# Chunked attention and a gated network: the next block's attention in two batches instead of four

## The chip, the cores and the metric

The kernel runs on one core of one Trainium2 chip. The metric is the time of one launch on the device in microseconds (us), lower is better. The engines that matter are TensorE (PE, matrix products into PSUM), VectorE (DVE), ScalarE (ACT) and the queues on which DMAs are issued: SyncE's (SP) for loads, and ACT's own for the output.

## The reference

Attention within chunks of 64 positions, for 8 batches, 8 heads, 576 positions and 64 numbers a head, then a gated feed-forward network on 4608 tokens of 512 numbers:

```python
scores = scale * np.matmul(q_c, k_c.transpose(0, 1, 2, 4, 3))
scores = scores - np.max(scores, axis=-1, keepdims=True)
attn = np.exp(scores)
attn = attn / (np.sum(attn, axis=-1, keepdims=True) + 1e-09)
out = np.matmul(attn, v_c)
...
g = x @ w_gate
silu = g * (1.0 / (1.0 + np.exp(-g)))
val = x @ w_val
return (silu * val @ w_out).astype(np.float32)
```

`w_gate` and `w_val` are 512 x 1536, `w_out` is 1536 x 512.

## The kernel before

The tokens are taken in nine blocks (b = 0 to 8) of 512. A block's attention covers four pairs of heads (p = 0 to 3). `Attn` holds it: `load_qk` loads a pair's q and k, `scores` (L180) makes their products in two PSUM tiles (h = 0, 1; a PSUM tile here is one bank of 128 x 512 numbers), takes the maximum of each row and writes the difference to `s` in SBUF, `exponents` (L201) and `normalize` (L206) finish the softmax in place, `turn` (L229) transposes it into the tile `turned` by DVE, `columns_crossed` (L242) multiplies with v into two banks and copies them back to `s` by ACT, and `ready` (L264) splits the result into two parts xh and xl, the operands of the feed-forward network. Each small product is 64 x 64; the program has 32 such instructions for two pairs, and the trace shows 64, since it lists each of these as two passes.

The network runs in twelve steps (f = 0 to 11) of 128 hidden columns. A step of a block is: `gate` (12 large matmuls into a bank of the pool `ps_gv`, silu by ACT, L292), `value` (12 more into the other bank of `ps_gv`), `times` (L299, DVE, reads the value's bank), the splitting of `h` into hh (ACT) and hl (DVE), L56 and L57, and 12 matmuls of `project` (L312) into four banks of `ps_o`. The pool `ps_gv` has two banks, `ps_a` two, `ps_o` four: all eight are taken. A product of three parts stands for each exact one (L273 to L275, L318 to L320). `lag` (L331) runs `project` one step late: the output product of step f-1 is emitted behind the gate and value of step f. So the previous block's step 11 is projected at f = 0 of the next block, and there ACT copies the four output tiles out (L325) and issues their DMAs (L327) on its own queue, each behind its copy.

The order on PE, ACT and DVE is the order in which the code is written. The order of SP's DMAs is set by a scheduler. From b = 2 on, `block` (L558) makes the attention of block b+1 between the steps of block b: `behind[f]` is called at the end of step f, `middle[f]` ahead of step f's output weights. Blocks 2 to 7 do this, six in all; blocks 0, 1 and 2 get their attention elsewhere, in code that the change leaves in its order.

```python
middle = {2: exponents}
behind = {0: lambda: scores(0), 1: lambda: scores(2), 3: normalize,
          4: lambda: turn(0, 0), 5: lambda: turn(0, 1),
          6: lambda: (values(0), turn(2, 0)),
          7: lambda: turn(2, 1), 8: lambda: nxt.ready(0, 2), 9: lambda: values(2), 10: lambda: nxt.ready(2, 2)}
```

`scores(p)` and `values(p)` each handle pairs p and p+1, in the two banks of `ps_a`. The loads of q and k use two buffers, `qk_t`, each for one pair; the staged h tiles of the pass ahead of block 2 (twelve late steps of block 1) use the same two. The v loads and two of the four output tiles share the buffers `v_t`.

Of the kernel before, what the change touches and what calls it, by code (L numbers as in the profile page):

```python
# [8 lines left out]
F32 = mybir.dt.float32  # L9
# [10 lines left out]
P = 128  # L20
C = 64
# [6 lines left out]
NP = H // 2  # L28
T = 4
# [6 lines left out]
def attn_then_gated_ffn(ctx: ExitStack, tc: tile.TileContext, qk, v, wgv, wo, out):  # L36
    nc = tc.nc
    const = ctx.enter_context(tc.tile_pool(name="const", bufs=1))
    ld = ctx.enter_context(tc.tile_pool(name="ld", bufs=2))
# [6 lines left out]
    ps_gv = ctx.enter_context(tc.tile_pool(name="ps_gv", bufs=2, space=bass.MemoryType.PSUM))  # L46
    ps_o = ctx.enter_context(tc.tile_pool(name="ps_o", bufs=T, space=bass.MemoryType.PSUM))
    ps_a = ctx.enter_context(tc.tile_pool(name="ps_a", bufs=2, space=bass.MemoryType.PSUM))
# [106 lines left out]
    class Attn:  # L155
# [12 lines left out]
                              in_=qk[:, p:p + n, self.b].rearrange("p n a k -> p n (a k)"))  # L168
            return t

        def load_v_crossed(self, p):

            t = ld.tile([P, 2, T, C], F32, name="v_t", tag="v_t")
            src = v[:, p, self.b].rearrange("p (c j) d -> p c j d", j=2)
            nc.sync.dma_start(out=t[:, 0], in_=src[:, :, 0])
            for h in range(2):
                nc.sync.dma_start(out=t[h * C:(h + 1) * C, 1], in_=src[(1 - h) * C:(2 - h) * C, :, 1])
            return t

        def scores(self, tiles, p, c=0, m=T, pool=ps_a, tag="ps_a"):  # L180

            n = sum(t.shape[1] for t in tiles)
            ps = [pool.tile([P, n, m, C], F32, name="ps_a", tag=tag) for _ in range(2)]
            i = 0
            for t in tiles:
                for k in range(t.shape[1]):
                    for u in range(2 * m):
                        j, us = u % 2, u % (2 * M) * C
                        for h in range(2):
                            r = slice(h * C, (h + 1) * C)  # L190
                            part = t[r, k, u // (2 * M)]
                            nc.tensor.matmul(ps[h][j * C:(j + 1) * C, i, u // 2, :], part[:, us:us + C],  # L192
                                             part[:, M * P + us:M * P + us + C], start=True, stop=True)
                    i += 1
            for h in range(2):
                top = small.tile([P, n, m, 1], F32, name="top")
                nc.vector.tensor_reduce(out=top, in_=ps[h], axis=AX.X, op=ALU.max)  # L197
                nc.vector.tensor_tensor(out=self.s[:, p:p + n, c:c + m, h], in0=ps[h],
                                        in1=top.broadcast_to([P, n, m, C]), op=ALU.subtract)
# [19 lines left out]
        def columns(self, v_t, pT, pool=ps_a, tag="ps_a"):  # L219

            pT = pT.rearrange("p (u k) -> p u k", k=C)
            px = pool.tile([P, 2 * T, C], F32, name="px", tag=tag)
            for u in range(2 * T):
                for h in range(2):
                    r = slice(h * C, (h + 1) * C)
                    nc.tensor.matmul(px[r, u, :], v_t[r, u, :], pT[r, u, :], start=True, stop=True)  # L226
            return px.rearrange("p u k -> p (u k)")

        def turn(self, p, j, parts=(0, 1)):  # L229


            if not hasattr(self, "turned"):
                self.turned = const.tile([P, NP, 2, T, C], F32, name="turned", tag="turned")
            src = self.s[:, p:p + 2].rearrange("p a c h k -> p (a c) h k")
            for i in (2 * j + i for i in parts):
                for o in range(4):
                    to = 32 * (o ^ 2 * j)
                    nc.vector.transpose(  # L238
                        out=self.turned[to:to + 32, p:p + 2, j, :, 32 * (i % 2):32 * (i % 2) + 32],
                        in_=src[32 * i:32 * i + 32, :, o // 2, 32 * (o % 2):32 * (o % 2) + 32])  # L240

        def columns_crossed(self, v_t, p, n):  # L242


            px = [ps_a.tile([P, n, T, C], F32, name="ps_a") for _ in range(2)]
            for i in range(n):
                for u in range(T):
                    for j in range(2):
                        for h in range(2):
                            r = (h ^ j) * C  # L250
                            nc.tensor.matmul(px[j][h * C:(h + 1) * C, i, u, :], v_t[i][r:r + C, j, u, :],  # L251
                                             self.turned[r:r + C, p + i, j, u, :], start=True, stop=True)
            for j in range(2):
                nc.scalar.copy(out=self.s[:, p:p + n, :, j], in_=px[j])
# [22 lines left out]
    def out_weights(f, engine=None):  # L277
        woh = wp.tile([P, DM], F32R, name="woh")
        wol = wp.tile([P, DM], F32R, name="wol")
        split(wo_raw[f], woh, wol, engine)  # L280
        return woh, wol
# [19 lines left out]
    def gated(a, f):  # L301
        h = gate(a, f)
        times(h, value(a, f))
        return h

    def parts(a, f, h):
        hh = hp.tile([P, N], F32R, name="hh")
        hl = hp.tile([P, N], F32R, name="hl")
        split(h, hh, hl)
        return a, f, hh, hl  # L310
# [20 lines left out]
    def lag(parts, wo_f):  # L331

        if pending:
            project(*pending.pop())
        if parts is not None:
            pending.append((parts, wo_f))

    def side(a):

        kept = {}  # L340

        def scores(p):
            a.scores([a.load_qk(p), a.load_qk(p + 1)], p)

        def exponents():
            kept["s"] = a.exponents(0, NP)

        def normalize():
            a.normalize(kept["s"])

        def turn(p, j, parts=(0, 1)):
            a.turn(p, j, parts)
            if j and 1 in parts:
                kept["v"] = [a.load_v_crossed(p + i) for i in range(2)]

        def values(p):
            a.columns_crossed(kept["v"], p, 2)

        return scores, exponents, normalize, turn, values
# [35 lines left out]
    def by_pe(a, pairs, v_t):  # L395
        for p in pairs:
            a.turn_by_pe(p, turned_by_pe[:, p])
        return [a.columns(v_t[p], turned_by_pe[:, p], ps_o, "ps_o") for p in pairs]
# [8 lines left out]
    px = by_pe(a0, (0, 1), v0)  # L407
# [26 lines left out]
    px = by_pe(a1, (0, 1), v1)  # L434
# [65 lines left out]
    def pT(p):  # L500
        return nxt.turned[:, p].rearrange("p j t k -> p (j t k)")
# [8 lines left out]
    def prepare(f):  # L510
        if f % 2 == 0:
# [14 lines left out]
    o.below()  # L526
    nxt = Attn(2)
    scores, exponents, normalize, turn, values = side(nxt)
    o.power()
    scores(0)  # L530
    o.weigh()
    o.join()
# [15 lines left out]
    behind = {1: lambda: turn(0, 0, (0,)), 2: lambda: (turn(0, 0, (1,)), nxt.turn_by_pe(2, pT(2))),  # L548
              3: lambda: (turn(0, 1, (0,)), columns(2), nxt.turn_by_pe(3, pT(3))),
              4: lambda: (columns(3), turn(0, 1, (1,))), 5: lambda: nxt.ready(2, 2),  # L550
              6: lambda: values(0), 8: lambda: nxt.ready(0, 2)}
# [6 lines left out]
    def block(a, b):  # L558
        nxt = Attn(b + 1) if b + 1 < NB else None
        middle, behind = {}, {}  # L560
        if nxt:
            scores, exponents, normalize, turn, values = side(nxt)
            middle = {2: exponents}
            behind = {0: lambda: scores(0), 1: lambda: scores(2), 3: normalize,
                      4: lambda: turn(0, 0), 5: lambda: turn(0, 1),
                      6: lambda: (values(0), turn(2, 0)),
                      7: lambda: turn(2, 1), 8: lambda: nxt.ready(0, 2), 9: lambda: values(2), 10: lambda: nxt.ready(2, 2)}
        for f in range(NF):
            wo_f = []

            def between():
                middle.get(f, lambda: None)()
                wo_f.extend(out_weights(f))

            h = gated(a, f)
            between()
            lag(parts(a, f, h), wo_f)
            behind.get(f, lambda: None)()
        return nxt

    a = nxt
    for b in range(2, NB):
        a = block(a, b)
# [34 lines left out]
```

## Time and profile before

| | us |
|---|---|
| median of 3 runs | 989.31 (988.85 to 989.68) |
| the profiled execution | 988.99 |
| its span, first to last instruction | 987.1 |
| PE busy in it | 952.7 |
| DVE busy | 513.5 |
| ACT busy | 337.7 |

The chain of work that ended last lies on PE for 91% of the span. The granted clock of PE has a mean of 0.991. A busy PE is not proof of PE at its peak, since matmuls are pipelined and overlap in the trace (a large one is listed with 0.39 us); the starts tell how far they stand apart.

### The profile page before, as it was taken

Reading aid. Unit: us, or ns where it says so; the run is one execution under the profiler, and the core shown is the slowest. Engines: PE = TensorE matmul, PEld = TensorE weight load, DVE = VectorE, ACT = ScalarE, POOL = GpSimd, SP = SyncE. Lnnn points to the kernel's source line nnn. Section 1 sums busy time; section 2 is a strip of 40 time slices with the busy share of each in tenths; the row PEclk is TensorE's granted clock in tenths of the full one; section 3 lists DMA queues with packets and bytes.
Section 4 is the critical chain, followed back from the end, with each engine's and each line's share of the span. In section 5 each row is a group of like instructions: output and inputs, shape, how many; then the busy total and the mean of one; then the engine's idle time right before and its main releaser. Section 6 shows DMA issues by size and latency. Waiting matters only on the chain.

```text
span 987.1 us, 14517 instructions
## 1 busy us (share of the span) xinstructions
PE 952.7 (97%) x6232; PEld 782.2 (79%) x6232; DVE 513.5 (52%) x816; ACT 337.7 (34%) x523; POOL 0.7 (0%) x6
## 2 busy tenths in 40 slices
PE   4689999999999999999999999999999999999998
PEld 4577888876888888888888888888888888888886
DVE  6777777758447524662356345633564347522221
ACT  3455444434532223222332323233322332223222
POOL 0000000000000000000000000000000000000000
PEclk9799999999999999999999999999999999999999
DMA  9061333235240005010401030002100120001001
GB/s 362 14 234 38 134 147 141 92 112 160 80 136 1 22 1 150 1 23 1 150 0 23 1 112 39 22 1 92 58 20 4 29 79 1 22 1 43 0 1 43
DMA packets 45600, 63.85 MB, mean 65 GB/s; under 512 B 29664, under 2 KB 29664, under 8 KB 44000
## 3 DMA queue, kind: packets, MB, share of 16 engines
q1 hardware_dynamic: 38624, 50.34, 15.8%
q10 hardware_dynamic: 6912, 12.59, 3.4%
q8 instruction: 49, 0.80, 0.3%
q14 instruction: 15, 0.12, 0.0%
HBM read 50.33 MB, written 12.58 MB: 64 GB/s over the span
## 4 chain that ended last, share of the span: by engine, by line
PE 91%; DVE 4%; DMA 2%; ACT 2%; issue 1%; ACTq 0%; SPq 0%; DVEq 0%
PE ps_gv L273 20%; PE ps_gv L274 19%; PE ps_gv L275 19%; PE ps_o L318 9%; PE ps_o L319 9%; PE ps_o L320 9%; DMA qk_t<-in_qk 2%; PE ps_a L192 2%; PE ps_a L251 1%; PE px L226 1%; DVE z L208 1%; DMA out<-o_sb 0%; DVE s_sb L211 0%; DVE t L81 0%; DVE t L97 0%
## 5 line engine op out<-in xcount | busy, mean ns | idle before, releaser
L273 PE MATMUL ps_gv<-xl,w 128*128 128x512 f32 x864 | 341.1, 395 | 3.4 <-ACT h L292 2.1
L274 PE MATMUL ps_gv<-xh,w 128*128 128x512 f32 x864 | 338.1, 391 | 3.2 <-DVE w L129 3.2
L275 PE MATMUL ps_gv<-xh,w 128*128 128x512 f32 x864 | 337.9, 391 | 0.0
L299 DVE SCALAR_TENSOR_TENSOR h<-ps_gv,h 128x512 f32<-128x512 f32 x108 | 74.6, 690 | 359.3 <-PE ps_gv L275 359.3
L273 PEld LDWEIGHTS ps_gv<-xl,w 128*128 128x128 f32 x864 | 163.0, 189 | 39.3 <-ACT h L292 2.5
L274 PEld LDWEIGHTS ps_gv<-xh,w 128*128 128x128 f32 x864 | 163.1, 189 | 36.9 <-DVE w L129 3.8
L275 PEld LDWEIGHTS ps_gv<-xh,w 128*128 128x128 f32 x864 | 163.0, 189 | 34.2
L292 ACT ACTIVATE h<-ps_gv 128x512 f32<-128x512 f32 x108 | 64.5, 597 | 315.0 <-PE ps_gv L275 314.9
L318 PE MATMUL ps_o<-woh,hl 128*128 128x512 f32 x432 | 169.9, 393 | 2.2 <-DVE hl L57 2.1
L319 PE MATMUL ps_o<-wol,hh 128*128 128x512 f32 x432 | 169.0, 391 | 0.0
L320 PE MATMUL ps_o<-woh,hh 128*128 128x512 f32 x432 | 168.9, 391 | 0.0
L56 ACT CAST hh<-h 128x512 fp32r<-128x512 f32 x96 | 59.6, 621 | 183.4 <-DVE h L299 183.4
L318 PEld LDWEIGHTS ps_o<-woh,hl 128*128 128x128 f32 x432 | 81.5, 189 | 21.1 <-issue 2.5
L319 PEld LDWEIGHTS ps_o<-wol,hh 128*128 128x128 f32 x432 | 81.6, 189 | 17.1 <-DVE wol L57 0.4
L320 PEld LDWEIGHTS ps_o<-woh,hh 128*128 128x128 f32 x432 | 81.5, 189 | 17.0
L238 DVE STREAM_TRANSPOSE turned<-s_sb 32x256 f32<-32x256 f32 x208 | 90.6, 436 | 3.1
L57 DVE TENSOR_TENSOR wol<-wo,woh 128x512 fp32r<-128x512 f32 x108 | 73.8, 683 | 12.8 <-ACT woh L56 12.8
L57 DVE TENSOR_TENSOR hl<-h,hh 128x512 fp32r<-128x512 f32 x96 | 66.4, 692 | 18.1 <-ACT hh L56 11.1
L56 ACT CAST woh<-wo 128x512 fp32r<-128x512 f32 x108 | 66.0, 611 | 11.1 <-DVE wo L97 11.1
L197 DVE TENSOR_REDUCE top<-ps_a 128x8 f32<-128x512 f32 x36 | 24.6, 685 | 36.1 <-PE ps_a L192 36.1
L192 PEld LDWEIGHTS ps_a<-qk_t 64*64 64x64 f32 x1152 | 20.4, 144 | 14.8 <-DMA qk_t<-in_qk 9.2
L192 PE MATMUL ps_a<-qk_t 64*64 64x64 f32 x1152 | 23.5, 232 | 8.8 <-DMA qk_t<-in_qk 8.4
(49 smaller groups left out, 438.7 us busy)
## 6 DMA issues: line engine op xcount, KB each, us to landing
qk_t<-in_qk SPq DMA_DIRECT2D x30, 512.0 KB, 4.5
raw<-in_wgv SPq DMA_DIRECT2D x12, 1024.0 KB, 7.0
out<-o_sb ACTq DMA_DIRECT2D x36, 256.0 KB, 2.3
raw<-in_wo SPq DMA_DIRECT2D x6, 1024.0 KB, 4.9
v_t<-in_v SPq DMA_DIRECT2D x26, 128.0 KB, 2.8
v_t<-in_v SPq DMA_DIRECT2D x52, 64.0 KB, 2.8
qk_t<-in_qk SPq DMA_DIRECT2D x3, 1024.0 KB, 13.8
h<-h ACTq DMA_DIRECT2D x12, 256.0 KB, 2.0
```

The source lines that it names most:

```text
L56: nc.scalar.copy(out=hi, in_=src)
L57: (engine or nc.vector).tensor_tensor(out=lo, in0=src, in1=hi.bitcast(F32), op=ALU.subtract)
L192: nc.tensor.matmul(ps[h][j * C:(j + 1) * C, i, u // 2, :], part[:, us:us + C], part[:, M * P + us:M * P + us + C], start=True, stop=True)
L238: nc.vector.transpose(out=self.turned[to:to + 32, p:p + 2, j, :, 32 * (i % 2):32 * (i % 2) + 32], in_=src[32 * i:32 * i + 32, :, o // 2, 3 ...
L273: nc.tensor.matmul(ps, wh, xl, start=k == 0, stop=False)
L274: nc.tensor.matmul(ps, wl, xh, start=False, stop=False)
L275: nc.tensor.matmul(ps, wh, xh, start=False, stop=k == n - 1)
L292: nc.scalar.activation(h, pg, AF.Silu, scale=2.0 ** -8)
L299: nc.vector.scalar_tensor_tensor(out=h, in0=pv, scalar=2.0 ** -8, in1=h, op0=ALU.mult, op1=ALU.mult)
L318: nc.tensor.matmul(o, hl[:, ts], woh, start=f == 0, stop=False)
L319: nc.tensor.matmul(o, hh[:, ts], wol, start=False, stop=False)
L320: nc.tensor.matmul(o, hh[:, ts], woh, start=False, stop=f == NF - 1)
```

## The change

In `block`, the scores of all four pairs are made at f = 0, and their values at f = 8. Pairs 0 and 1 use the two banks of `ps_gv`, pairs 2 and 3 those of `ps_a`. The scores in `ps_gv` are copied to `s` by ACT (`take`) and reduced from there; those in `ps_a` are reduced from PSUM as before. Pairs 2 and 3 of q and k are loaded by one DMA into the buffer of `turned`, and v of pairs 2 and 3 into the two buffers `qk_t`, both at other times of the block than their usual holders.

```diff
+        def take(self, ps, p):
+            to = [self.s[:, p:p + ps[0].shape[1], :, h] for h in range(2)]
+            for h in range(2):
+                nc.scalar.copy(out=to[h], in_=ps[h])
+            return to
...
-        def columns_crossed(self, v_t, p, n):
-            px = [ps_a.tile([P, n, T, C], F32, name="ps_a") for _ in range(2)]
+        def columns_crossed(self, v_t, p, n, pool=ps_a, tag="ps_a"):
+            px = [pool.tile([P, n, T, C], F32, name="ps_a", tag=tag) for _ in range(2)]
...
-            scores, exponents, normalize, turn, values = side(nxt)
+            _, exponents, normalize, _, _ = side(nxt)
+            kept_v = []
+            def scores():
+                tiles = [nxt.load_qk(0), nxt.load_qk(1)], [nxt.load_qk(2, 2, const, "turned")]
+                ps = nxt.products(tiles[0], pool=ps_gv, tag="ps_gv"), nxt.products(tiles[1])
+                nxt.less_top(nxt.take(ps[0], 0), 0)
+                nxt.less_top(ps[1], 2)
+            def load_v():
+                kept_v.extend(nxt.load_v_crossed(p, "v_t" if p < 2 else "qk_t") for p in range(NP))
+            def values():
+                nxt.columns_crossed(kept_v[:2], 0, 2, ps_gv, "ps_gv")
+                nxt.columns_crossed(kept_v[2:], 2, 2)
             middle = {2: exponents}
-            behind = {0: lambda: scores(0), 1: lambda: scores(2), 3: normalize,
-                      4: lambda: turn(0, 0), 5: lambda: turn(0, 1),
-                      6: lambda: (values(0), turn(2, 0)),
-                      7: lambda: turn(2, 1), 8: lambda: nxt.ready(0, 2), 9: lambda: values(2), 10: lambda: nxt.ready(2, 2)}
+            behind = {0: scores, 3: normalize, 4: lambda: turn(0, 0), 5: lambda: turn(0, 1),
+                      6: lambda: (turn(2, 0), load_v()), 7: lambda: turn(2, 1),
+                      8: values, 9: lambda: nxt.ready(0, 2), 10: lambda: nxt.ready(2, 2)}
```

`products` and `less_top` are the two halves of the former `scores`; `load_v_crossed` takes the buffer's tag as a further argument.

How instructions move on ACT at f = 0 of block 3 (o_sb are the output tiles, h the result of the silu of f = 1, s_sb the scores of block 4; numbers tell buffers apart). Before:

```order
L325 ACTIVATE o_sb_3132<-ps_o_2383 128x512
L327 DMA out_0<-o_sb_3132 128x512
L292 ACTIVATE h_3192<-ps_gv_3179 128x512
L56 CAST woh_3208<-wo1_639 128x512
L56 CAST hh_3212<-h_3192 128x512
```

After:

```order
L339 ACTIVATE o_sb_3132<-ps_o_2427 128x512
L341 DMA out_0<-o_sb_3132 128x512
L204 COPY s_sb_3073<-ps_a_3141 128x8x64
L204 COPY s_sb_3073<-ps_a_3142 128x8x64
L306 ACTIVATE h_3236<-ps_gv_3223 128x512
L56 CAST woh_3252<-wo1_639 128x512
```

The two new copies (their tiles are called ps_a, but lie in `ps_gv`) stand behind the last output tile's copy and DMA issue and ahead of the silu of f = 1.

How they move on PE at the same place, f = 0 of block 3. Before:

```order
L319 MATMUL ps_o<-wol,hh 128x512
L320 MATMUL ps_o<-woh,hh 128x512
L192 MATMUL ps_a<-qk_t 64x64 x32
L273 MATMUL ps_gv<-xl_2875,w 128x512
L274 MATMUL ps_gv<-xh_2874,w 128x512
```

After:

```order
L333 MATMUL ps_o<-wol,hh 128x512
L334 MATMUL ps_o<-woh,hh 128x512
L195 MATMUL ps_a<-qk_t 64x64 x64
L287 MATMUL ps_gv<-xl_2960,w 128x512
L288 MATMUL ps_gv<-xh_2959,w 128x512
```

The batch of 32 has become one of 64, between the same output product and the gate of f = 1; the batch at f = 1 is gone. At f = 8 there is one of 64 too, in place of those at f = 6 and f = 9.

How loads move on SP ahead of block 2 (h_in are the staged h tiles). Before:

```order
L513 DMA h_in_2183<-h10_1672 128x1024
L167 DMA qk_t_2299<-in_qk 128x1024
L167 DMA qk_t_2301<-in_qk 128x1024
L167 DMA qk_t_2396<-in_qk 128x1024
L175 DMA v_t_2659<-in_v 128x4x64
L167 DMA qk_t_2398<-in_qk 128x1024
```

After:

```order
L527 DMA h_in_2183<-h10_1672 128x1024
L167 DMA qk_t_2303<-in_qk 128x2x1024
L167 DMA qk_t_2299<-in_qk 128x1024
L167 DMA qk_t_2301<-in_qk 128x1024
L175 DMA v_t_2724<-in_v 128x4x64
```

Pairs 2 and 3 come as one load, ahead of pairs 0 and 1, and no v load stands between them any more.

More of the change, by code (lines that the diff above doesn't have):

```diff
@@ L169, in load_qk, with load_v_crossed @@
             return t
-        def load_v_crossed(self, p):
-            t = ld.tile([P, 2, T, C], F32, name="v_t", tag="v_t")
+        def load_v_crossed(self, p, tag="v_t"):
+            t = ld.tile([P, 2, T, C], F32, name="v_t", tag=tag)
             src = v[:, p, self.b].rearrange("p (c j) d -> p c j d", j=2)
@@ L180, in scores, with products @@
         def scores(self, tiles, p, c=0, m=T, pool=ps_a, tag="ps_a"):
+            self.less_top(self.products(tiles, c, m, pool, tag), p, c)
+        def products(self, tiles, c=0, m=T, pool=ps_a, tag="ps_a"):
             n = sum(t.shape[1] for t in tiles)
@@ L194, in scores, with less_top @@
                     i += 1
+            return ps
+        def take(self, ps, p):
[3 more added lines that the diff above has]
+            return to
+        def less_top(self, ps, p, c=0):
+            n, m = ps[0].shape[1:3]
             for h in range(2):
@@ L561, in block, with turn @@
         if nxt:
-            scores, exponents, normalize, turn, values = side(nxt)
-            middle = {2: exponents}
-            behind = {0: lambda: scores(0), 1: lambda: scores(2), 3: normalize,
-                      4: lambda: turn(0, 0), 5: lambda: turn(0, 1),
-                      6: lambda: (values(0), turn(2, 0)),
-                      7: lambda: turn(2, 1), 8: lambda: nxt.ready(0, 2), 9: lambda: values(2), 10: lambda: nxt.ready(2, 2)}
+            _, exponents, normalize, _, _ = side(nxt)
[10 more added lines that the diff above has]
+                nxt.columns_crossed(kept_v[2:], 2, 2)
+            middle = {2: exponents}
+            behind = {0: scores, 3: normalize, 4: lambda: turn(0, 0), 5: lambda: turn(0, 1),
+                      6: lambda: (turn(2, 0), load_v()), 7: lambda: turn(2, 1),
+                      8: values, 9: lambda: nxt.ready(0, 2), 10: lambda: nxt.ready(2, 2)}
+            def turn(p, j):
+                nxt.turn(p, j)
         for f in range(NF):
```

## The prediction, made before the changed kernel had run

> **What bounds the kernel now.** I read the page's span and chain first, then the busy time over one block, then the chain in order of time for what repeats in a block, then TensorE's (PE's) own timeline around a batch of small products.
>
> ```profile
> span 987.1 us, 14517 instructions
> PE 91%; DVE 4%; DMA 2%; ACT 2%; issue 1%; ACTq 0%; SPq 0%; DVEq 0%
> ```
>
> The chain that ended last lies on PE for 91% of the span. The view by windows, for one whole block of 512 tokens (first column the stretch, then its length, then the busy time of PE with the number of instructions), shows that inside a block PE has no gap at all:
>
> ```profile
> 374.88:478.08 103.20, 103.20 (x695) 84.91 (x689) 50.32 (x84) 31.79 (x52) 0.00 (x0) 1.00 0.15 42
> ```
>
> DVE (50.32) and ScalarE, called ACT (31.79), have much room. So a block is the sum of PE's pieces, and the change must be read there. The chain in order of time shows the four batches of the next block's attention (start, duration): two of L192 (scores, f=0 and f=1) and two of L251 (values, f=6 and f=9).
>
> ```profile
> 373.85 1.09 PE ps_a L192 x64
> 383.33 1.09 PE ps_a L192 x64
> 425.45 1.09 PE ps_a L251 x64
> 451.25 1.09 PE ps_a L251 x64
> ```
>
> Now PE's timeline at one f=0 (start, duration, line; a duration includes the drain, so I go by starts):
>
> ```profile
> 473.72 0.39 PE L274 MATMUL ps_gv<-xh,w 128*128 128x512 f32 x1
> ...
> 476.67 0.39 PE L320 MATMUL ps_o<-woh,hh 128*128 128x512 f32 x1
> 476.98 1.16 PE L192 MATMUL ps_a<-qk_t 64*64 64x64 f32 x64
> 478.08 0.50 PE L273 MATMUL ps_gv<-xl,w 128*128 128x512 f32 x1
> ...
> 478.88 0.39 PE L273 MATMUL ps_gv<-xl,w 128*128 128x512 f32 x1
> ```
>
> From 473.72 to 476.67 thirteen large matmuls start, 0.227 apart. From the last large one before the batch (476.67, below "t0") to the first behind it (478.08) are 1.41, and the three after that take 0.80 instead of 0.68. So a batch costs 1.41 - 0.227 + 0.12 = 1.30 us. Sum of a block: 432 x 0.227 + 4 x 1.30 = 103.3, against 103.20 in the window. Nothing else is in it.
>
> **What merging saves.** How much of the 1.30 goes away when two batches stand back to back? The first block has a batch that a late load cut in two:
>
> ```profile
> 279.11 0.39 PE L320 MATMUL ps_o<-woh,hh 128*128 128x512 f32 x1
> 279.42 0.69 PE L192 MATMUL ps_a<-qk_t 64*64 64x64 f32 x32
> 280.54 0.69 PE L192 MATMUL ps_a<-qk_t 64*64 64x64 f32 x32 [0.42 <-DMA qk_t<-in_qk]
> 281.16 0.50 PE L273 MATMUL ps_gv<-xl,w 128*128 128x512 f32 x1
> ```
>
> 32 passes take 0.69, 64 take 1.16: 0.47 for 32 more, so 0.94 for 64 more. A batch of 128 costs 1.30 + 0.94 = 2.24 instead of 2.60: 0.36 us saved by each merge. Two merges a block in six blocks (b = 2 to 7; the last has no next block) are 12 x 0.36 = 4.3 us. Bounds: 0.2 to 0.4 each (64 passes that need a whole 1.09 more, or nothing left of the switch but the 0.94).
>
> The same rows give the third term: here 279.11 to 281.16 are 2.05 instead of 1.41, so PE lost 0.64 us to the load of pair 3. Afterwards all loads of that block stand ahead of the v loads in SP's order, and the last of them waits only for the last staged h tile, whose last reader is this row on DVE; a load of 512 KB lands 4.5 us after its issue, one of 1 MB 13.8:
>
> ```profile
> 259.83 0.69 DVE L57 TENSOR_TENSOR hl<-h_in,hh 128x512 fp32r<-128x512 f32 x1 [1.43 <-ACT hh L56]
> ...
> qk_t<-in_qk SPq DMA_DIRECT2D x30, 512.0 KB, 4.5
> ...
> qk_t<-in_qk SPq DMA_DIRECT2D x3, 1024.0 KB, 13.8
> ```
>
> 260.5 + 4.5 = 265, ahead of the batch at 269.9. The 1 MB load is issued before that, when `turned` comes free at the sixth of twelve steps. So 0.64 us is won once. In later blocks the loads are released at f=8, three steps of 8 us before their use, and the v loads at f=0, eight steps ahead: nothing waits.
>
> **What the new place costs.** The first two pairs' products now fill both banks of `ps_gv`. The next gate product (f=1) writes the first of them and must wait until ACT has copied it out. At f=0 ACT also empties the previous block's four output tiles (L325), each followed by a DMA issue on the same queue (L327), and the new copies stand behind all of them. ACT's timeline at the same f=0:
>
> ```profile
> 475.69 0.59 ACT L325 ACTIVATE o_sb<-ps_o 128x512 f32<-128x512 f32 x1
> ...
> 477.48 0.34 ACTq L327 DMA_DIRECT2D out<-o_sb  x1
> 477.92 0.60 ACT L325 ACTIVATE o_sb<-ps_o 128x512 f32<-128x512 f32 x1 [0.47 <-PE ps_a L192]
> 478.55 0.34 ACTq L327 DMA_DIRECT2D out<-o_sb  x1
> 479.06 0.60 ACT L325 ACTIVATE o_sb<-ps_o 128x512 f32<-128x512 f32 x1 [0.55 <-ACT o_sb L325]
> 479.69 0.41 ACTq L327 DMA_DIRECT2D out<-o_sb  x1
> 481.13 0.60 ACT L292 ACTIVATE h<-ps_gv 128x512 f32<-128x512 f32 x1 [1.47 <-PE ps_gv L275]
> ```
>
> The last issue ends at 480.10, t0 + 3.43, long after PE left the output product. Today nothing waits for that: the next thing on ACT is the silu at 481.13. Of the six blocks one is later, with t0 = 373.47 and the last issue over at 377.13, t0 + 3.66; the other five lie close to the first.
>
> ```profile
> 373.47 0.39 PE L320 MATMUL ps_o<-woh,hh 128*128 128x512 f32 x1
> ...
> 376.79 0.34 ACTq L327 DMA_DIRECT2D out<-o_sb  x1
> ```
>
> The copy itself I price by the copy of the same shape (589 ns), and the hand-over from ACT to PE by a place where PE waited for ACT (75.47 to 75.52: 0.05):
>
> ```profile
> L254 ACT COPY s_sb<-ps_a 128x512 f32<-128x512 f32 x26 | 14.0, 589 | 28.7 <-PE ps_a L251 28.7
> ```
>
> ```profile
> 74.87 0.60 ACT h L292
> 75.52 0.50 PE ps_gv L273
> ```
>
> So: 480.10, + 0.10 (from an issue's end to the next ACT instruction that has nothing to wait for, 477.82 to 477.92), + 0.59, + 0.05 = 480.84. Without the wait the gate would start at 478.08 + 0.94 = 479.02. PE stands still 1.82 us; in the late block 377.13 + 0.74 - (373.47 + 2.35) = 2.05. Five times 1.82 and once 2.05 are 11.2 us. Bounds for one wait: 1.6 (no gap, output copies a little earlier) to 2.05. The second copy ends half a microsecond later and serves the value product, 2.7 us behind the gate: no wait.
>
> The same question at f=8, where values of pairs 0 and 1 go to `ps_gv`: there ACT has no output tiles, and starts its copies at once:
>
> ```profile
> 528.58 1.16 PE L251 MATMUL ps_a<-turned,v_t 64*64 64x64 f32 x64
> 529.67 0.50 PE L273 MATMUL ps_gv<-xl,w 128*128 128x512 f32 x1
> ...
> 529.78 1.07 ACT L254 COPY s_sb<-ps_a 128x512 f32<-128x512 f32 x2 [2.39 <-PE ps_a L251]
> ```
>
> The first copy ends at 529.78 + 0.59 = 530.37, and the second half of the batch runs until 529.67 + 0.94 = 530.61. Covered by 0.2 us, so nothing; that cover is thin.
>
> DVE takes on no more instructions than before, only all at f=0. A pair's four (two reductions, two subtractions) took 478.20 to 480.93:
>
> ```profile
> 478.20 0.69 DVE L197 TENSOR_REDUCE top<-ps_a 128x8 f32<-128x512 f32 x1 [1.69 <-PE ps_a L192]
> ...
> 480.24 0.69 DVE L198 TENSOR_TENSOR s_sb<-ps_a,top 128x512 f32<-128x512 f32 x1
> ```
>
> Two such groups from 480.8 end at 486.2; the gated product that DVE makes next needs the value product of f=1, which ends at about 480.84 + 24 x 0.227 = 486.3, and the output product that reads it stands two more products away. Hidden. The turns, which now end at f=7, have all of f=8's gate and value ahead of the batch. The 12 more copies on ACT (two a block) cost PE nothing but the wait above.
>
> **Sum.** - 4.3 - 0.64 + 11.2 = + 6.2 us. The profiled execution took 988.99 us (span 987.1); the median of the runs shown is 989.31, 0.3 above. 989.3 + 6.2 = 995.5 us.
>
> **The clock.** PE's clock is the first rival. The windows view around two gaps, cut into stretches of 3.41 us such that the halved one is whole (behind the length the busy time of PE; third from the end, 1.00 or 0.50, the granted clock):
>
> ```profile
> 71.65:75.07 3.42, 1.76 (x8) 1.13 (x6) 2.70 (x6) 1.73 (x4) 0.00 (x0) 1.00 0.00 0
> 75.07:78.48 3.41, 2.96 (x13) 2.45 (x14) 3.34 (x5) 0.39 (x1) 0.00 (x0) 1.00 0.00 0
> 208.17:211.59 3.42, 1.45 (x65) 1.25 (x65) 2.45 (x4) 1.14 (x2) 0.00 (x0) 1.00 0.70 264
> 211.59:215.00 3.41, 3.41 (x9) 2.73 (x9) 2.67 (x4) 0.00 (x0) 0.00 (x0) 0.50 0.55 166
> ```
>
> After a stretch with 1.76 busy the clock stayed; after one with 1.45 it was halved for the next 3.41 us. The new gap, from the end of the 128 passes (476.98 + 1.16 + 0.94 = 479.08) to 480.84, is 1.76, so a stretch that holds it whole has 3.41 - 1.76 = 1.65 busy: between the two, nearer to the one that stayed. I therefore take no loss of clock. If it is lost, each time costs half of 3.41 = 1.7 us, and a stretch of 3.41 laid anywhere holds a gap of 1.76 whole in (3.41 - 1.76) / 3.41 = 48% of cases: three blocks of six, + 5.1, 1000.6 us. The Trainium skill ("TensorE: Matmul & The Clock Gate", section "Why this matters for your kernels") says that only gaps of more than about 3 us between bursts bring the clock down. By that rule this rival could not happen and the sum stays 995.5; the trace does not agree with it, since the stretch 208.17:211.59 was idle for 3.42 - 1.45 = 1.97 us in all and was followed by 0.50.
>
> **Other rivals.** Faster: the gate at f=1 finds its bank empty, because ACT's output tiles are through before the products end. For it: today PE has no gap whatever; against it: the last issue would have to end by 479.02 - 0.74 = 478.28, and it ends at 480.10. Time: 989.3 - 4.3 - 0.64 = 984.4. Dearer wait: the gate waits for both copies, not one. The pair takes 1.07 (row at 529.78), 0.48 more than one: 6 x 0.48 at f=0, and at f=8 529.78 + 1.07 + 0.05 - 530.61 = 0.29, six times: + 4.6, 1000.1. Against it: the copies are two instructions, each with its own bank. About the same: ACT's output copies shift so that half of the wait goes (0.9 each): 989.3 - 4.9 + 5.6 = 990.0; nothing in the rows moves them.
>
> **How the numbers follow.** 0.52 for the sum as it stands (its own range, by the bounds of the wait and the merges, 993.5 to 998); 0.30 for the lost clock (997 to 1003 for one to five blocks); 0.08 for the dearer wait; 0.05 for faster; 0.05 for about the same. Range 992.5 to 1001.5. A measurement of this kernel can tell about 0.2%, 2 us, from no change: faster 0.06, same 0.05, slower 0.89.
>
> **What would show it.** In the trace after: batches of 128 passes, from t0 to the next large matmul 4.1 to 4.4 us at f=0 with the gate idle for the copy on ACT, and about 2.35 at f=8 with no wait; a block of 104.3 us; no wait for a qk load in the first block; a clock of 1.00 through f=1. Wrong if ACT reaches its copies earlier than the fourth output's issue, or if rows at 0.50 follow f=0.

## The result and the profile after

The changed kernel took 995.91 us (median of 13 runs, 989.8 to 1000.7), against 989.31 of the kernel before: ratio 1.0058, 95% interval 1.0037 to 1.0079. In a second comparison, on another occasion, the medians were 995.47 (6 runs) and 988.69, ratio 1.0082 (1.0058 to 1.0107). By the two intervals it is slower by about 4 to 11 us. The forecast was 995.5 us.

The profiled execution took 995.91 us. First its span and chain, as of before:

```profile
span 994.0 us, 14491 instructions
PE 89%; DVE 4%; ACT 3%; DMA 2%; ACTq 1%; issue 1%; SPq 0%; DVEq 0%
```

ACT and its queue, which made 2% and 0% of the chain, now make 3% and 1%. One block by windows (the stretch, its length, the busy time of PE; third from the end the granted clock), and PE at its f=0 and f=8:

```profile
380.10:484.19 104.09, 102.59 (x689) 84.88 (x689) 50.24 (x85) 32.62 (x54) 0.00 (x0) 1.00 0.13 41
```

```profile
376.18 0.39 PE L334 MATMUL ps_o<-woh,hh 128*128 128x512 f32 x1
376.49 2.10 PE L195 MATMUL ps_a<-qk_t 64*64 64x64 f32 x128
380.10 0.50 PE L287 MATMUL ps_gv<-xl,w 128*128 128x512 f32 x1 [1.51 <-ACT s_sb L204]
...
445.32 0.39 PE L334 MATMUL ps_o<-woh,hh 128*128 128x512 f32 x1
445.64 2.11 PE L265 MATMUL ps_a<-turned,v_t 64*64 64x64 f32 x128
447.68 0.50 PE L287 MATMUL ps_gv<-xl,w 128*128 128x512 f32 x1
```

PE, without a gap in a block before, is now idle for 104.09 - 102.59 = 1.50 us in each. The row at 380.10 says for whom: the gate of f=1 waits for ACT's copy, L204. From the last output matmul to the gate are 3.92 us at f=0 and 2.36 at f=8, where nothing waits. The wait is therefore worth 3.92 - 2.36 = 1.56 us. ACT at the same place:

```profile
375.20 0.59 ACT L339 ACTIVATE o_sb<-ps_o 128x512 f32<-128x512 f32 x1
...
378.45 0.60 ACT L339 ACTIVATE o_sb<-ps_o 128x512 f32<-128x512 f32 x1 [0.47 <-ACT o_sb L339]
379.08 0.34 ACTq L341 DMA_DIRECT2D out<-o_sb  x1
379.46 1.07 ACT L204 COPY s_sb<-ps_a 128x512 f32<-128x512 f32 x2 [0.41 <-ACT o_sb L339]
```

The products end at 378.59; the copy starts at 379.46, behind the fourth output tile and its DMA issue. Taken over the blocks, one is 104.06 long on average against 103.20, + 0.86, six times + 5.2. The first block's load of q and k is no longer waited for, - 0.64: its batch is one piece of 128 passes.

```profile
272.40 2.10 PE L195 MATMUL ps_a<-qk_t 64*64 64x64 f32 x128
```

That makes + 4.5, and from the first block's last output matmul to the end the two traces differ by just that: 987.1 - 269.63 = 717.5 before, 994.0 - 272.08 = 721.9 after. The rest of the 6.9 us between the spans lies ahead of this place, in code whose order on PE, ACT and DVE did not change. The windows view up to it, of before and of after:

```profile
0.00:269.63 269.63, 240.41 (x1696) 196.05 (x1696) 189.72 (x279) 124.79 (x177) 0.70 (x6) 0.97 0.38 137
```

```profile
0.00:272.08 272.08, 243.92 (x1695) 198.66 (x1696) 189.66 (x279) 124.88 (x177) 0.70 (x6) 0.96 0.38 140
```

It took 2.45 us more at a granted clock of 0.96 instead of 0.97. The 2.45 us are there already at a load of v that SP issues at 241.31 before and at 243.76 after, ahead of the first load whose order changed. The time of a single run goes with its mean clock: in 27 runs of the kernel before it lay between 984.89 us (clock 0.994) and 991.42 (0.988). So a difference of a few us needs either many runs or the length of a block, which hardly depends on this.

### The profile page after: what moved, and what is told of

Same layout as the page of the kernel before. It is cut to its first block, busy times and chain, and to the rows that moved or that the text cites. A ratio compares the mean times of both kernels' runs of the same rounds, so it can differ in the third digit from the quotient of the medians.

```text
span 994.0 us, 14491 instructions
## 1 busy us (share of the span) xinstructions
PE 952.1 (96%) x6232; PEld 784.5 (79%) x6232; DVE 512.9 (52%) x816; ACT 343.8 (35%) x535; POOL 0.7 (0%) x6
## 4 chain that ended last, share of the span: by engine, by line
PE 89%; DVE 4%; ACT 3%; DMA 2%; ACTq 1%; issue 1%; SPq 0%; DVEq 0%
PE ps_gv L287 20%; PE ps_gv L288 19%; PE ps_gv L289 19%; PE ps_o L332 9%; PE ps_o L333 9%; PE ps_o L334 9%; ACT o_sb L339 2%; PE ps_a L265 1%; DMA qk_t<-in_qk 1%; ACTq L341 1%; PE px L240 1%; DVE z L222 1%; PE ps_a L195 1%; DVE s_sb L225 0%; DVE t L81 0%
## 5 line engine op out<-in xcount | busy, mean ns | idle before, releaser
L339 ACT ACTIVATE o_sb<-ps_o 128x512 f32<-128x512 f32 x36 | 21.5, 597 | 15.0 <-PE ps_o L334 6.9
```

## The experiments

Theory A was that of the prediction: the merges save what was worked out, and the price is the wait for a copy that stands behind the output tiles on ACT. Theory B: a bank of the first product is dear wherever and by whomever it is emptied. Theory D: the clock.

**Scores at f=1.**

```diff
-            behind = {0: scores, 3: normalize, 4: lambda: turn(0, 0), 5: lambda: turn(0, 1),
+            behind = {1: scores, 3: normalize, 4: lambda: turn(0, 0), 5: lambda: turn(0, 1),
```

> Only the step of the scores changes: all four pairs' scores at f = 1 instead of f = 0, where ScalarE has no output tiles. Theory A (the wait of 1.56 us for ScalarE's copy behind the output tiles is the whole price): from the last output matmul to the gate 2.36 us instead of 3.92, a block of 102.5 us instead of 104.06, the kernel 5 us under the one before (984 to 985). Theory B (the price is in the bank, wherever the scores stand): the gate of f = 2 waits too, block about 104. Theory C (the exponents, now 1 step behind the scores instead of 2, wait for VectorE): ScalarE about 2 us late at f = 2, without effect on TensorE.

Median 985.21 us, ratio 0.9963 (0.9947 to 0.9980). A block, and PE, ACT at f=1, then ACT at f=2:

```profile
381.87:484.33 102.46, 102.46 (x693) 84.88 (x695) 50.23 (x84) 32.62 (x53) 0.00 (x0) 1.00 0.14 42
```

```profile
381.80 2.10 PE L195 MATMUL ps_a<-qk_t 64*64 64x64 f32 x128
383.83 0.50 PE L287 MATMUL ps_gv<-xl,w 128*128 128x512 f32 x1
...
383.02 1.07 ACT L204 COPY s_sb<-ps_a 128x512 f32<-128x512 f32 x2 [2.41 <-PE ps_a L195]
...
389.05 1.92 ACT L217 ACTIVATE s_sb<-s_sb 128x2048 f32<-128x2048 f32 x1 [0.26 <-DVE s_sb L212]
```

The same copy of the same bank, one step later: it starts while PE is still in the batch, and PE has no gap. Theory A holds, B falls as to the place. Theory C was oversized: ACT waited 0.26 us for DVE, not 2.

**Copies by DVE.**

```diff
-                nc.scalar.copy(out=to[h], in_=ps[h])
+                nc.vector.tensor_copy(out=to[h], in_=ps[h])
```

> Scores stay at f = 0; the two copies out of the first product's banks are made by VectorE instead of ScalarE. Theory A: VectorE is idle there, copies at once, 0.7 us behind the first half of the batch, so the gate does not wait: block 102.5 us. Theory B (a bank that has to be copied costs whichever engine does it): block 104.

Median 982.90 us, ratio 0.9947 (0.9927 to 0.9967). A block by windows, then DVE and ACT at f=0:

```profile
371.18:473.62 102.44, 102.44 (x692) 84.86 (x696) 51.42 (x86) 31.74 (x52) 0.00 (x0) 1.00 0.14 42
```

```profile
372.32 1.29 DVE L204 COPY s_sb<-ps_a 128x512 f32<-128x512 f32 x2 [1.68 <-PE ps_a L195]
...
374.01 0.34 ACTq L341 DMA_DIRECT2D out<-o_sb  x1
```

DVE starts the first of its two copies at 372.32, when ACT still has two output tiles ahead of it (its last issue is at 374.01). Here ACT's lateness remains, and nobody on PE's path waits for it. The rest of B falls.

**Output DMAs from SP's queue.**

```diff
-                nc.scalar.dma_start(out=out[r:r + P, :], in_=o_sb)
+                nc.sync.dma_start(out=out[r:r + P, :], in_=o_sb)
```

> As the changed kernel, but the output tiles' DMAs are issued from SyncE's queue instead of ScalarE's, for all blocks. Theory A (ScalarE is late because a DMA issue stands behind each output copy): the last output copy ends at about t0 + 1.1, the copy out of the bank starts with the end of its products, t0 + 1.5, no wait: block 102.5 us. Rival (the output copies alone make ScalarE late): a wait of 0.5 us or more stays, block over 103.

Median 982.90 us, ratio 0.9943 (0.9924 to 0.9963). A block by windows, and ACT at f=0:

```profile
374.31:476.79 102.48, 102.48 (x693) 84.88 (x694) 50.24 (x84) 32.27 (x54) 0.00 (x0) 1.00 0.14 42
```

```profile
372.95 2.05 ACT L339 ACTIVATE o_sb<-ps_o 128x512 f32<-128x512 f32 x4
375.51 1.07 ACT L204 COPY s_sb<-ps_a 128x512 f32<-128x512 f32 x2 [0.51 <-PE ps_a L195]
```

The four output copies now take 2.05 us together, where in the changed kernel they took 3.85 (375.20 to 379.05) with three issues between them. ACT is idle for 0.51 us ahead of the bank's copy and waits for PE. So the lateness came from the DMA issues, not from the output copies alone.

**No copies.**

```diff
-                nxt.less_top(nxt.take(ps[0], 0), 0)
+                nxt.less_top(ps[0], 0)
```

> Scores stay at f = 0; the reduction and subtraction read the first product's banks directly, no copies. The first bank is free after two VectorE instructions (1.35 us) instead of one copy. Theory A: the gate waits until t0 + 1.51 + 1.35 + 0.05 = t0 + 2.91 instead of t0 + 2.36, a wait of 0.55 us, block 103.05 us. Theory B: block 104.

Median 987.17 us, ratio 0.9981 (0.9961 to 1.0001): by time not told apart from the kernel before. Its block, then DVE and PE at f=0:

```profile
374.70:477.87 103.17, 102.49 (x692) 84.85 (x695) 50.22 (x84) 31.74 (x52) 0.00 (x0) 1.00 0.14 42
```

```profile
375.84 0.69 DVE L211 TENSOR_REDUCE top<-ps_a 128x8 f32<-128x512 f32 x1 [1.68 <-PE ps_a L195]
376.57 0.69 DVE L212 TENSOR_TENSOR s_sb<-ps_a,top 128x512 f32<-128x512 f32 x1
...
377.40 0.47 PE L287 MATMUL ps_gv<-xl,w 128*128 128x512 f32 x1 [0.68 <-DVE s_sb L212]
```

The two DVE instructions hold the bank for 1.42 us (375.84 to 377.26), where one copy takes 0.59. So the gate waits, for 0.68 us; 0.55 was expected. The two instructions were to take 1.35 us and the gate to start 0.05 behind them, where it starts 0.14 behind. The wait eats the saving of the two merges: a block of 103.17 against 103.20.

**Values merged alone, scores merged alone.** Each restores the former pieces of the other half; `scores2`, `turn1` and `values1` are the former functions, for two pairs at a time:

```diff
# values only
...
-            behind = {0: scores, 3: normalize,
+            behind = {0: lambda: scores2(0), 1: lambda: scores2(2), 3: normalize,
...
# scores only
...
-                      6: lambda: (turn(2, 0), load_v()), 7: lambda: turn(2, 1),
-                      8: values, 9: lambda: nxt.ready(0, 2), 10: lambda: nxt.ready(2, 2)}
+                      6: lambda: (values1(0), turn1(2, 0)),
+                      7: lambda: turn1(2, 1), 8: lambda: nxt.ready(0, 2), 9: lambda: values1(2), 10: lambda: nxt.ready(2, 2)}
```

> Only the values are merged (f = 8, pairs 0 and 1 in the first product's banks); the scores stay in two batches at f = 0 and f = 1 as before the change. Theory A (each merge saves 0.33 to 0.36 us, no wait at f = 8): block 102.85 us, the kernel 2.1 us under the one before. Rival (merging saves nothing, the 128 passes cost twice 64): block 103.2.

> Only the scores are merged (f = 0); the values stay in two batches at f = 6 and f = 9. Theory A: the merge saves 0.35 us a block, the wait costs 1.56: block 103.20 - 0.35 + 1.56 = 104.4 us, the slowest of all. Theory B (the values' merge holds part of the loss): block under 104.06.

Medians 986.76 us, ratio 0.9973 (0.9957 to 0.9989), and 1000.27 us, ratio 1.0123 (1.0086 to 1.0160). A block of the first, then one of the second:

```profile
369.62:472.45 102.83, 102.83 (x693) 84.87 (x695) 50.33 (x84) 31.77 (x52) 0.00 (x0) 1.00 0.15 42
```

```profile
377.02:481.59 104.57, 102.92 (x693) 84.85 (x694) 50.24 (x84) 32.70 (x54) 0.00 (x0) 1.00 0.14 41
```

A merge alone is worth 103.20 - 102.83 = 0.37 us. In two other blocks of that trace the batch at f=1 waited for a load of q and k, which made the block 0.69 and 0.40 us longer; why was not tried. The scores alone give 1.65 us of idle and 104.57, 0.2 over the expectation. All of this block's loss sits at f=0. And in this trace the wait is not always the same:

```profile
587.62 1.16 ACTq L341 DMA_DIRECT2D out<-o_sb  x1
...
590.63 0.50 PE L287 MATMUL ps_gv<-xl,w 128*128 128x512 f32 x1 [2.48 <-ACT s_sb L204]
```

Here a DMA issue took 1.16 us instead of 0.34, and PE waited 2.48. Three of the six waits are so long (2.27, 2.48 and 2.50), each behind an issue of 1.14 to 1.19 us, and behind two of them the clock was halved for a stretch of 3.41 us. The windows at the row above:

```profile
588.61:592.02 3.41, 1.39 (x6) 1.17 (x7) 1.38 (x3) 1.67 (x3) 0.00 (x0) 1.00 0.93 315
592.02:595.43 3.41, 3.41 (x10) 2.62 (x9) 3.31 (x6) 0.42 (x1) 0.00 (x0) 0.50 0.79 213
```

Six blocks of 104.57 would make about + 8 us, and the median is 11.6 above that of the kernel before. Such waits and losses can hold the rest, but for the runs without a trace this is not shown.

**The changed kernel again, and a longer gap.** For the second, the first bank is copied three times:

```diff
-            for h in range(2):
+            for h in (0, 0, 0, 1):
                 nc.scalar.copy(out=to[h], in_=ps[h])
```

> The changed kernel once more, for a second trace and more times. Its 13 times lay between 989.8 and 1000.7 us. Theory A: the six waits at f = 0 are of 1.5 us in every run, block 104.06, and what differs between runs is the granted clock in the part ahead of block 2, which the change leaves in its order. Theory D: the waits differ from run to run, or the clock is lost behind them in some runs; then this trace has rows at 0.50 behind f = 0, or blocks of another length.

> As the changed kernel, but the first bank is copied three times, so that the gate of f = 1 waits 1.0 us longer and TensorE is idle for about 2.5 us. Theory A with the clock held in any case (only gaps of over 3 us count): block 105.1 us. Theory with the clock lost (a stretch of 3.41 us with less than 1.45 to 1.76 busy): rows at 0.50 behind f = 0 in those blocks whose gap lies whole or nearly so in one stretch, each of them 1.7 us longer, blocks of 105.1 and of 106.8 us.

The repeated kernel's times are given above. Four of its six waits are about as in the first trace (1.50 to 1.58 us of idle), two are longer, 1.92 and 1.94: the fourth issue took 0.75 and 0.80 us there. Behind the 1.92 the clock was lost. Rows of ACT's queue, of PE, and windows before and behind, in this trace:

```profile
795.19 0.75 ACTq L341 DMA_DIRECT2D out<-o_sb  x1
...
796.62 0.49 PE L287 MATMUL ps_gv<-xl,w 128*128 128x512 f32 x1 [1.92 <-ACT s_sb L204]
...
797.54 0.63 PE L287 MATMUL ps_gv<-xl,w 128*128 128x512 f32 x1
```

```profile
793.96:797.37 3.41, 1.49 (x55) 1.27 (x47) 0.74 (x2) 1.80 (x4) 0.00 (x0) 0.98 0.90 279
797.37:800.78 3.41, 3.41 (x9) 2.63 (x9) 3.34 (x6) 0.00 (x0) 0.00 (x0) 0.52 0.46 109
```

With 1.49 us busy in that stretch the clock was halved in the next. The gap of 1.94 fell on two stretches, with 2.42 and 2.46 us busy, and the clock stayed. In the first trace the gap of 1.51 lies whole in a stretch too, with 1.90 busy, and the clock stays:

```profile
377.69:381.10 3.41, 1.90 (x68) 1.62 (x58) 0.99 (x2) 1.96 (x4) 0.00 (x0) 1.00 0.90 269
381.10:384.51 3.41, 3.41 (x16) 2.79 (x15) 3.34 (x6) 1.11 (x2) 0.00 (x0) 1.00 0.58 140
```

So theory A's second half (the same waits in every run, the clock lost only ahead of block 2) is refuted, and D holds in part. The longer gap took 1007.11 us (2 runs; ratio 1.0196, 1.0151 to 1.0240). PE in two of its blocks:

```profile
384.78 0.79 PE L287 MATMUL ps_gv<-xl,w 128*128 128x512 f32 x1 [2.74 <-ACT s_sb L204]
385.37 0.63 PE L288 MATMUL ps_gv<-xh,w 128*128 128x512 f32 x1
385.80 0.63 PE L289 MATMUL ps_gv<-xh,w 128*128 128x512 f32 x1
...
491.41 0.50 PE L287 MATMUL ps_gv<-xl,w 128*128 128x512 f32 x1 [2.74 <-ACT s_sb L204]
491.75 0.40 PE L288 MATMUL ps_gv<-xh,w 128*128 128x512 f32 x1
491.99 0.40 PE L289 MATMUL ps_gv<-xh,w 128*128 128x512 f32 x1
```

The first of the two goes on at half speed (0.43 from start to start), the second, with the same idle time, at full speed (0.24). Three of six lost the clock. In none of the three does the gap lie whole in one stretch; what tells them from the others is how much of it does. Below are the stretches around the first, cut at its change of the clock (384.22), then those of another block (gap of 2.81) where the clock stayed. The latter are counted on from there: the changes at 384.22 and 701.66 are 93 stretches of 3.413 us apart.

```profile
380.81:384.22 3.41, 1.23 (x85) 1.09 (x76) 0.00 (x0) 2.45 (x5) 0.00 (x0) 1.00 0.79 234
384.22:387.63 3.41, 2.85 (x7) 2.27 (x8) 2.80 (x5) 0.99 (x2) 0.00 (x0) 0.50 0.53 142
592.43:595.84 3.41, 1.57 (x108) 1.43 (x100) 0.00 (x0) 2.08 (x4) 0.00 (x0) 1.00 0.85 270
595.84:599.26 3.42, 2.46 (x11) 2.02 (x12) 2.41 (x4) 1.36 (x3) 0.00 (x0) 1.00 0.56 139
```

The three losses have 0.49, 1.12 and 1.23 us busy in the stretch ahead of them, the other three blocks 1.57 or more. Extra copies cost 0.62 each, not 0.50, hence a gap of 2.74 instead of 2.5 in most blocks.

Nothing beats the versions with copies by DVE and with output DMAs from SP, both at 982.90 us and, by the intervals above, 0.3 to 0.8% under the kernel before.

## Why the prediction was right

- **The place of the wait**: right. The gate of f=1 waits for L204 in all six blocks of both traces, and moving the step, the engine or the DMA issues takes the wait away each time (102.44 to 102.48 instead of 104.06).
- **The size of the wait**: 1.82 us foretold, 1.56 in the first trace. The fourth output tile started 2.27 behind t0 instead of 2.39, its issue took 0.34 instead of 0.41, and the copy followed 0.04 behind it instead of 0.10: 0.25 us together. In the second trace two waits were about 2.0. The single late block of before (2.05) did not come back in its place.
- **The merges**: 2.35 us from the last large matmul to the next foretold, 2.36 measured; 0.36 a merge against 0.37 in the kernel with the values alone.
- **f=8**: hidden, as foretold; the gate follows the batch at once (447.68).
- **The load in the first block**: won, 0.64 us.
- **The sum**: + 6.2 foretold (waits of 11.2, savings of 4.3 and 0.64), + 4.5 by the blocks in the first trace, where the waits make 9.4, and 995.8 - 271.6 - 717.5 = + 6.7 in the second, with two long waits and one loss of clock. The first trace's span reached 994.0 also by 2.45 us ahead of block 2, which no step of the prediction holds. How much of the median's difference of 6.6 us comes from long waits and lost clock in the runs that left no trace is not known. That the median came out within 0.4 us of the forecast is partly luck.
- **The clock**: held behind all six waits of the first trace, as the forecast took it; but the rival is real. It needs about 1.9 us of idle time within one stretch, 0.4 more than the usual wait, and got it once in the second trace. The 1.65 us busy of the foretold wait would not have been enough for it: the clock stayed behind 1.57. The rule of the Trainium skill that was weighed ("TensorE: Matmul & The Clock Gate", section "Why this matters for your kernels", only gaps of more than about 3 us) does not agree with the gap of 1.92 us.
- **Faster, same, the dearer wait**: none occurred. The gate waits for one copy alone: it starts 0.05 behind the first copy's end (379.46 + 0.59 to 380.10), ahead of the second's (380.53).

## What to carry to other kernels

When a product is to borrow a bank from the next large product, ask which engine empties it and what stands ahead of that emptying in the engine's queue at that very step; an engine that is 34% busy over the span can still be two microseconds late at one place. DMA issues between short copies nearly double the time that a queue needs (3.85 us instead of 2.05 for four copies), so give them to a queue that no copy on the critical path shares. Two merged batches save only the switch between them, 0.37 us here, so a wait of 0.4 us undoes a merge.

## What the runs showed of the hardware

- The clock of PE is lost after far less than a whole idle stretch: with 1.39 and 1.49 us busy of 3.41 the next stretch ran at half speed, with 1.57, 1.76 and 1.90 it did not. So a gap of 2.74 us counts only by the part of it that falls into one stretch.
- A DMA issue on ACT's queue, 0.34 us mostly, took 0.56 to 1.36 at the same place in some blocks of the traces; in the kernel before it was 0.64 once, where nothing on PE's path waited for it. A load on SP's queue was under way at most of these issues, but also at issues of 0.34, and at the one of 1.19 there was none; why is open and was not tried.
- The mean granted clock of a run, settled for the most part in the first 240 us of the traces, goes with its time: 984.89 us at 0.994 and 991.42 at 0.988, without any change of code.
